# State update as 48-column tiles, and the state's output product as 64-row tiles in two PSUM banks

## The chip, the cores and the metric

One core of one Trainium2 chip. The metric is the device time of one execution in microseconds (us); lower is better. All runs that are compared are at a granted TensorE clock of 1.0 (0.997 to 0.999 in some executions).

## The reference

A gated linear attention over 4 batches, 8 heads, 768 tokens and head dimension D = 48, and after it a feed-forward block with a hard-swish:

```python
for t in range(S):
    state = alpha[:, :, t, :, None] * state + einsum('bhd,bhe->bhde', k[:, :, t], v[:, :, t])
    y[:, :, t] = einsum('bhd,bhde->bhe', q[:, :, t], state)
x = y.transpose(0, 2, 1, 3).reshape(3072, 384)
h = x @ w_in                        # 384 -> 2048
g = h * clip(h + 3, 0, 6) / 6
out = g @ w_out                     # 2048 -> 384
```

Everything is float32.

## The kernel before

The tokens go in 24 chunks of 128 (six per batch). Inside a chunk the recurrence is done by matrix products; between chunks a 48x48 state per head is carried on. Heads lie in pairs: on the 128 rows of a tile, head 0 of a pair has rows 0 to 47 and head 1 rows 64 to 111 (the rest is padding). Per chunk TensorE computes scores, an output product inside the chunk (`within`), the state's output product (`across`) and the state update (`update`). These are small against the feed-forward products around them, which fill most of the time.

```python
def bank(name, j):              # four PSUM banks in rotation, shared by all of these
    ps_t[name, j] = ps.tile([C, NP, C], FP, tag="t", bufs=4, name=name + "_ps")
    return ps_t[name, j]

def update(j):                  # 4 products, one per pair of heads: 128 columns by 96
    # ... (u is a bank seen as NP x 96 columns)
    for p in range(NP):
        one = vs[:, 2 * p]
        both = bass.AP(one.tensor, one.offset, [one.ap[0], (C - D, 2), (1, D)])
        nc.tensor.matmul(u[:, p], kb_t[j][:, p], both, start=True, stop=True)

def next_state(j):              # VectorE takes only the two diagonal 48x48 blocks of each pair
    # ...

def across(j):                  # 12 products in four tiles of 32 columns, all 128 rows
    # ...
    for n in range(KT * NP):
        kk, p = divmod(n, NP)
        nc.tensor.matmul(ps_t["y", j][32 * p : 32 * p + 32, kk],
                         st[j % 2][:, p, 32 * kk : 32 * kk + 32], Q_t[j][:, p],
                         start=False, stop=(kk == KT - 1), skip_group_check=True)

def keep_x(j):                  # ScalarE copies the output to SBUF
    # ...
    nc.scalar.copy(out=xT_t[g][:, :, (j % G) * C : (j % G + 1) * C],
                   in_=ps_t.pop(("y", j))[:, 0:KT])
```

The order of all instructions is written down by hand, as a string of some 1,600 words: `u.7` is the update of chunk 7, `yi.7` and `yx.7` its two output products, `st.8` the decayed state for chunk 8, `z` are filler products that keep TensorE busy during the start, `M`, `P`, `f` are the feed-forward.

```python
with tc.manual_schedule():
    run("""z.3.6 lk.0 lq.0 la.0 la.1 tk.0 w.1 tq.0 ta.0 ca.0 ta.1 r.0 z.0.18 ca.1 ...
```

## Time and profile before

| | before |
|---|---|
| time, median of 3 | 582.42 us (581.78 to 582.7) |
| span of the profiled execution | 579.1 us |
| TensorE busy | 568.0 us, 98% |
| TensorE instructions | 5112 |

The lines that show TensorE as the bound are in the prediction. The waits of TensorE (who waited for whom: us in total, times, longest):

```profile
PE m_ps L461 <- DVE ones L114: 4.2, 1, 4.2
PE ta_ps L267 <- DMA rings<-in_alpha_dram: 1.1, 1, 1.1
```

The first filler waits for the constant tile that it multiplies, and a transpose of an input (into `ta_ps`; `tk_ps` and `tq_ps` are others) for its transfer. The start has about 1.5 us more of such waits, and after it there is hardly any. The second is the timeline near 60 us (start, length, engine, line):

```profile
58.16 1.66 POOL L207 TENSOR_TENSOR w<-raw 128x768 int32<-128x768 int32 x1 [3.22 <-DVE raw L202]
...
59.00 1.13 PE L367 MATMUL u_ps<-t,kb 128*128 128x96 f32 x8
...
59.96 1.70 PE L420 MATMUL m_ps<-xT,w 128*128 128x256 f32 x7
```

GpSimd's last step on a weight piece ends at 58.16 + 1.66 = 59.82 us. The product that uses it starts at 59.96, and that product's weight load, which reads the piece, already at 59.88. There is no wait in the list, but the piece was only 0.14 us early for the product, and 0.06 us for its load.

### The profile page before, as it was taken

What the parts mean: (1) busy time and instruction counts of PE and PEld (TensorE: products, weight loads), DVE (VectorE), ACT (ScalarE), POOL (GpSimd) and SP (SyncE); (2) the same over time, 40 slices, a digit from 0 to 9 for tenths busy, and PEclk for the clock granted to TensorE, in tenths of its full rate; (3) what the DMA queues carried; (4) which work ended last, traced back from release to release, by engine and by line L of the source; (5) the groups of instructions that cost most, each with busy time, mean ns of one, the idle gap of its engine ahead of it and who ended that gap; (6) DMA issues with size and microseconds to landing.
All of it is one profiled execution on the core that took longest, in us unless ns stands there. A gap on an engine that the chain in (4) does not pass through costs nothing.

```text
span 579.1 us, 12352 instructions
## 1 busy us (share of the span) xinstructions
PE 568.0 (98%) x5112; PEld 531.3 (92%) x5112; DVE 473.4 (82%) x787; ACT 194.9 (34%) x335; POOL 53.2 (9%) x70
## 2 busy tenths in 40 slices
PE   6899999999999999999999999999999999999997
PEld 6788877699999999999999999999999999999997
DVE  5889889999999999895997886984998975655571
ACT  2346552103522523323323422422431431432420
POOL 2252435000000000000000000000000000000000
PEclk9999999999999999999999999999999999999999
DMA  9999797105115143440431331232242000000000
GB/s 166 202 177 211 213 236 177 37 23 140 33 40 141 28 99 75 97 103 8 97 79 32 78 90 40 58 96 54 48 113 46 16 23 8 1 22 8 3 18 28
DMA packets 87607, 45.83 MB, mean 79 GB/s; under 512 B 48896, under 2 KB 82432, under 8 KB 87552
## 3 DMA queue, kind: packets, MB, share of 16 engines
q1 hardware_dynamic: 80928, 40.33, 32.5%
q10 hardware_dynamic: 6624, 4.72, 2.4%
q8 instruction: 40, 0.66, 0.5%
q14 instruction: 15, 0.12, 0.1%
HBM read 40.30 MB, written 4.72 MB: 78 GB/s over the span
## 4 chain that ended last, share of the span: by engine, by line
PE 90%; DVE 4%; DMA 3%; SPq 2%; issue 1%; ACT 0%; DVEq 0%
PE m_ps L630 34%; PE m_ps L530 30%; PE m_ps L420 7%; PE sc_ps L325 4%; PE m_ps L446 4%; PE y_ps L389 3%; PE y_ps L399 2%; PE u_ps L367 2%; PE kb_ps L342 1%; DMA rings<-in_alpha_dram 1%; DMA raw<-in_moe_w_in_dram 1%; SPq L172 1%; DVE g_sb L428 1%; SPq L235 1%; DVE P L305 1%
## 5 line engine op out<-in xcount | busy, mean ns | idle before, releaser
L630 PE MATMUL m_ps<-w,g_sb 128*128 128x192 f32 x704 | 121.8, 328 | 0.5 <-DVE g_sb L467 0.3
L630 PEld LDWEIGHTS m_ps<-w,g_sb 128*128 128x128 f32 x704 | 113.7, 190 | 3.3 <-DVE g_sb L467 1.2
L536 ACT COPY g_sb<-m_ps 128x512 f32<-128x512 f32 x110 | 64.1, 584 | 118.3 <-PE m_ps L530 103.9
L630 PE MATMUL m_ps<-rings,g_sb 128*128 128x192 f32 x528 | 91.4, 326 | 0.5 <-DVE oh L646 0.5
L630 PEld LDWEIGHTS m_ps<-rings,g_sb 128*128 128x128 f32 x528 | 85.7, 190 | 0.8 <-DVE oh L646 0.7
L530 PE MATMUL m_ps<-xc,w 128*128 128x128 f32 x640 | 83.0, 277 | 0.3 <-DVE xc L467 0.3
L530 PEld LDWEIGHTS m_ps<-xc,w 128*128 128x128 f32 x640 | 77.8, 192 | 2.4 <-issue 1.8
L424 ACT ACTIVATE r<-g_sb,half 128x512 f32<-128x512 f32 x80 | 57.1, 723 | 60.6 <-DVE g_sb L469 22.6
L428 DVE SCALAR_TENSOR_TENSOR g_sb<-r,g_sb 128x512 f32<-128x512 f32 x80 | 55.4, 702 | 22.1 <-PE m_ps L630 13.5
L352 POOL TENSOR_TENSOR t<-t,R 128x384 f32<-128x384 f32 x20 | 19.4, 971 | 390.1 <-DVE t L379 213.9
L530 PE MATMUL m_ps<-xT,raw 128*128 128x128 f32 x400 | 52.8, 279 | 0.0
L530 PEld LDWEIGHTS m_ps<-xT,raw 128*128 128x128 f32 x400 | 48.4, 192 | 1.3
L530 PE MATMUL m_ps<-xT,w 128*128 128x128 f32 x320 | 44.1, 281 | 0.0
L420 PE MATMUL m_ps<-xT,w 128*128 128x256 f32 x192 | 43.6, 382 | 0.2 <-ACT xT L407 0.2
L577 DVE TENSOR_TENSOR g_sb<-g_sb 128x512 f32<-128x512 f32 (+1 forms) x55 | 41.9, 794 | 0.1
L530 PEld LDWEIGHTS m_ps<-xT,w 128*128 128x128 f32 x320 | 38.7, 191 | 3.2 <-ACT g_sb L536 1.4
L331 DVE TENSOR_TENSOR A<-sc_ps,mask 128x512 f32<-128x512 f32 x48 | 30.8, 684 | 12.5 <-PE sc_ps L325 12.4
L420 PEld LDWEIGHTS m_ps<-xT,w 128*128 128x128 f32 x192 | 35.8, 190 | 5.6 <-issue 0.4
L294 DVE TENSOR_TENSOR_SCAN R<-t,ones 128x516 f32<-128x516 f32 x24 | 29.4, 1224 | 8.0 <-ACT t L285 5.0
L530 PE MATMUL m_ps<-xc,raw 128*128 128x128 f32 x240 | 32.0, 276 | 0.0
L305 DVE TENSOR_TENSOR_SCAN P<-t 128x516 f32<-128x516 f32 x24 | 30.6, 1275 | 0.1
L467 DVE TENSOR_TENSOR g_sb<-g_sb 128x512 f32<-128x512 f32 x40 | 28.1, 703 | 2.9 <-ACT g_sb L536 2.6
(100 smaller groups left out, 714.1 us busy)
## 6 DMA issues: line engine op xcount, KB each, us to landing
raw<-in_moe_w_out_dram SPq DMA_DIRECT2D x8, 768.0 KB, 4.9
raw<-in_moe_w_in_dram SPq DMA_DIRECT2D x24, 192.0 KB, 6.9
t<-in_v_dram SPq DMA_DIRECT2D x48, 96.0 KB, 2.9
out_dram<-oh ACTq DMA_DIRECT2D x44, 96.0 KB, 2.2
qq<-in_q_dram SPq DMA_DIRECT2D x36, 96.0 KB, 2.4
aq<-in_alpha_dram SPq DMA_DIRECT2D x36, 96.0 KB, 2.5
kq<-in_k_dram SPq DMA_DIRECT2D x36, 96.0 KB, 2.5
qq<-in_q_dram SPq DMA_DIRECT2D x36, 80.0 KB, 2.5
```

Source lines behind the costliest of these rows:

```text
L294: nc.vector.tensor_tensor_scan(out=reverse(R, n - 1, n), data0=reverse(ax, n, n), data1=reverse(ones, n, n), initial=0.0, op0=ALU.mult, op ...
L305: nc.vector.tensor_tensor_scan(out=P_t[j], data0=aX[j % 2][:, 0:n], data1=ini[j % 2], initial=0.0, op0=ALU.mult, op1=ALU.add)
L325: nc.tensor.matmul(sc[h % 2][:, h // 2], K_t[j][r, h // 2], Q_t[j][r, h // 2], start=True, stop=True)
L331: nc.vector.tensor_tensor(out=A_t[j][:, NP * o : NP * (o + 1)], in0=ps_t.pop(("sc%d" % o, j)), in1=mask.unsqueeze(1).to_broadcast([C, NP, ...
L420: nc.tensor.matmul(h[:, f], w1[:, kk, o : o + C], xT_t[g][:, kk], start=(kk == 0), stop=(kk == KT - 1))
L424: nc.scalar.activation(out=to, in_=h, func=AF.Relu, bias=half, scale=1.0 / 6.0)
L428: nc.vector.scalar_tensor_tensor(out=to, in0=r, scalar=1.0, in1=h, op0=ALU.min, op1=ALU.mult)
L467: eng.tensor_tensor(out=out, in0=in0, in1=in1, op=ALU.add if s1 > 0 else ALU.subtract)
L530: nc.tensor.matmul(acc[g][i][:, f * C : (f + 1) * C], spots[w][:, f * C : (f + 1) * C], x_of(g, x), start=(first and f == 0), stop=last, s ...
L536: nc.scalar.copy(out=slots[z], in_=acc[g][i])
L577: nc.vector.tensor_tensor(out=out, in0=in0, in1=in1, op=ALU.subtract)
L630: nc.tensor.matmul(to[g], a, rhs[:, f], start=(first and f == 0), stop=(last and f == HF - 1), skip_group_check=True)
```

## The change

The intent: the update computes 128x96 per pair of heads, of which only two 48x48 blocks are used. Now it computes just these, as two column tiles side by side. In the state's output product, the outer thirds of the output belong to one head each, so half of their rows are zeros. Now they are 64 rows high, two above each other, in different PSUM banks (`y0` and `y1`). The middle third stays at full height. The copy to SBUF becomes two, and the order string was written anew.

```diff
     def update(j):
         for p in range(NP):
-            one = vs[:, 2 * p]
-            both = bass.AP(one.tensor, one.offset, [one.ap[0], (C - D, 2), (1, D)])
-            nc.tensor.matmul(u[:, p], kb_t[j][:, p], both, start=True, stop=True)
+            for a in range(2):
+                nc.tensor.matmul(u[64 * a : 64 * a + D, p, D * a : D * a + D],
+                                 kb_t[j][:, p, 64 * a : 64 * a + D],
+                                 vs[:, 2 * p + a, (64 - D) * a : (64 - D) * a + D],
+                                 start=True, stop=True)
...
+    def y_of(j, kk, p):
+        return ps_t["y%d" % (kk // 2), j][32 * p : 32 * p + 32, kk % 2]
...
     def across(j):
-        for n in range(KT * NP):
-            kk, p = divmod(n, NP)
-            nc.tensor.matmul(ps_t["y", j][32 * p : 32 * p + 32, kk],
-                             st[j % 2][:, p, 32 * kk : 32 * kk + 32], Q_t[j][:, p],
-                             start=False, stop=(kk == KT - 1), skip_group_check=True)
+        parts = [(p, 2 * a, slice(64 * a, 64 * a + 64)) for p in range(NP) for a in range(2)]
+        for p, kk, r in parts + [(p, 1, slice(0, C)) for p in range(NP)]:
+            nc.tensor.matmul(y_of(j, kk, p), st[j % 2][r, p, 32 * kk : 32 * kk + 32],
+                             Q_t[j][r, p], start=False, stop=(kk > 0), skip_group_check=True)
...
     def keep_x(j):
-        nc.scalar.copy(out=xT_t[g][:, :, (j % G) * C : (j % G + 1) * C],
-                       in_=ps_t.pop(("y", j))[:, 0:KT])
+        at = xT_t[g][:, :, (j % G) * C : (j % G + 1) * C]
+        nc.scalar.copy(out=at[:, 0:2], in_=ps_t.pop(("y0", j))[:, 0:2])
+        nc.scalar.copy(out=at[:, 2], in_=ps_t.pop(("y1", j))[:, 0])
...
-        run("""z.3.6 lk.0 lq.0 la.0 la.1 tk.0 w.1 tq.0 ta.0 ca.0 ta.1 r.0 z.0.18 ca.1 ...
+        run("""lk.0 lq.0 la.0 la.1 tk.0 w.1 tq.0 ta.0 ca.0 ta.1 r.0 z.0.18 ca.1 ...
         # the whole string is new, with 10 filler products fewer (30 instead of 40)
```

## The prediction

> **What bounds the kernel now.** I read the page first (shares, slices, chain), then the stretches by window, then TensorE's groups by form, and last its timeline in a steady part.
>
> ```profile
> PE 568.0 (98%) x5112; PEld 531.3 (92%) x5112; DVE 473.4 (82%) x787; ACT 194.9 (34%) x335; POOL 53.2 (9%) x70
> PE   6899999999999999999999999999999999999997
> DVE  5889889999999999895997886984998975655571
> PE 90%; DVE 4%; DMA 3%; SPq 2%; issue 1%; ACT 0%; DVEq 0%
> ```
>
> The reader is to see a TensorE that hardly ever stands still: it is 90% of the chain that ended last and fills every slice but the first and the last. ScalarE has two thirds of its time free. VectorE is less comfortable than its 82% looks, which the stretches show (columns: PE, PEld, DVE, ACT, POOL busy, then clock and DMA):
>
> ```profile
> 0.00:30.00 30.00, 22.94 (x254) 21.08 (x255) 22.09 (x40) 10.18 (x14) 8.18 (x26) 1.00 1.11 186
> 30.00:130.00 100.00, 100.00 (x728) 81.79 (x727) 91.54 (x129) 39.44 (x57) 30.28 (x30) 1.00 0.69 153
> 130.00:180.00 50.00, 49.71 (x445) 47.63 (x444) 49.74 (x88) 17.07 (x31) 2.08 (x2) 1.00 0.36 87
> 180.00:225.00 45.00, 45.00 (x461) 43.26 (x460) 43.53 (x75) 14.66 (x26) 1.67 (x2) 1.00 0.36 82
> 450.00:495.00 45.00, 45.00 (x432) 43.40 (x429) 33.25 (x61) 14.01 (x26) 1.67 (x2) 1.00 0.06 15
> ```
>
> The first 30 us are a start in which TensorE is idle for 7 us and also runs filler products. From 130 to 225 us both TensorE and VectorE are full (VectorE 49.74 of 50, then 43.53 of 45). Later TensorE alone is.
>
> The three groups that the change touches or leans on, in the view by form (busy time, then the mean of one):
>
> ```profile
> L367 PE MATMUL u_ps<-t,kb 128*128 128x96 f32 x160 | 21.0, 274 | 0.2 <-ACT kb L347 0.2
> L399 PE MATMUL y_ps<-q,t 128*32 128x128 f32 x480 | 17.2, 277 | 0.0
> L389 PE MATMUL y_ps<-A,t 128*32 128x128 f32 x768 | 25.9, 275 | 0.0
> ```
>
> Each float32 product stands as two instructions (80 products of the state update are x160). The means of 274 to 277 ns include the pipeline and are no cost. The cost is the distance from start to start, which the timeline gives (start, length, line, count):
>
> ```profile
> 229.78 1.03 PE L367 MATMUL u_ps<-t,kb 128*128 128x96 f32 x8
> 230.65 2.02 PE L530 MATMUL m_ps<-xc,w 128*128 128x128 f32 x16
> 232.60 1.08 PE L389 MATMUL y_ps<-A,t 128*32 128x128 f32 x32
> 233.62 1.16 PE L530 MATMUL m_ps<-xT,w 128*128 128x128 f32 x8
> 234.70 0.86 PE L399 MATMUL y_ps<-q,t 128*32 128x128 f32 x24
> 235.50 1.16 PE L530 MATMUL m_ps<-xT,w 128*128 128x128 f32 x8
> 236.49 2.77 PE L630 MATMUL m_ps<-w,g_sb 128*128 128x192 f32 x16
> ...
> 245.19 1.05 PE L530 MATMUL m_ps<-xc,w 128*128 128x128 f32 x8
> 246.08 0.39 PE L530 MATMUL m_ps<-xc,raw 128*128 128x128 f32 x2
> ```
>
> The update takes about 0.87 to 0.89 us for 8, so 111 ns each. That is the pace of a 128-column weight load (eight of L530 from 245.19 to 246.08: 0.89 us), not of its 96 moving columns. The two tiled groups take 1.02 us for 32 and 0.80 us for 24. Their difference, 0.22 us for two rounds of four, says that four column tiles run together and a round costs 109 ns. What is left over (1.02 - 8 x 0.109 = 0.15 us), plus what the L530 group before and after a tiled group takes above 0.89 us (1.08 before one, 0.99 between the last and L630), gives about 0.33 us for going into a tiled group and out again.
>
> **What the Trainium skill says.** (1) "TensorEngine Tiling (Array Packing)", Key Properties: changing the tiling mode, not only the tile, drains TensorE. The trace agrees: the first weight load of a new mode starts 0.20 us after the last 128-column product started, against 0.11 us inside a mode; so a drain costs about 95 ns beyond the stream. (2) "TensorE: Matmul & The Clock Gate", LDWEIGHTS: the load's time follows the number of columns P, about P/1.2 ns, whatever the rows. 128 columns give 107, the trace's pace is 111; 48 columns give an estimate of 40 ns, which nothing in this trace shows. (3) The tiling page, Gotcha 1, says that different row tiles cannot use one PSUM bank at the same time; this explains the second bank, and no run here shows it yet. (4) Its section Instruction Overhead puts about 60 cycles on each matmul; if that were a floor of some 50 ns (60 columns at the trace's 0.83 ns), a 48-column product would not quite scale.
>
> **The change part by part.** The order of the changed kernel's instructions, compared engine by engine, gives the counts.
>
> State update. Removed: 4 products of 128 weight columns by 96. Added: 8 of 48 by 48, in two column tiles. Before: 8 instructions x 111.7 = 0.894 us per chunk. After: 16 instructions in 8 rounds of two. A round is estimated at 48 x 0.83 + 5 = 45 ns (weights and stream both 40, the second load under the first product), so 0.36 us. For 20 chunks: 17.9 to 7.2, -10.7 us.
>
> Output product of the state. Before 6 rounds of 109 = 0.654 us per chunk. After: 8 half-height tiles of 64 rows by 32 columns together (2 rounds, if rows and columns combine), then the middle third at full height (2 rounds): 0.436 us. For 20 chunks -4.4 us. That row tiles combine is shown by the score products, whose 16 half-height instructions take 1.09 us with both changes of mode, so they run in pairs.
>
> Changes of mode. I counted them in both orders: 131 before, 182 after. Returns to the whole array go from 65 to 76; each costs 95 + 107 - 3 = 0.199 us, since the first 128-column load lies bare: +2.2 us. New entries into 64x32 tiles: 20 x (95 + 27) = +2.4 us. New entries into 128x64 tiles: 20 x (95 + 40) = +2.7 us. Together +7.3 us. The entries to the 32-column mode stay at 42, because the middle third is a new entry each time but the outer thirds take over the old one.
>
> Sum on TensorE: -10.7 - 4.4 + 7.3 = -7.8 us. As a check, the same counting (rounds, loads and changes, without idle) gives 562.9 us for the kernel before; its span is 579.1, 9.3 of the missing 16 us lie before 30 us and about 3 are spread over the rest.
>
> What doesn't reach the end: in the first 30 us TensorE waits for others anyway, so two updates and one output product there don't count (-0.8 us of gain). From 130 to 225 us VectorE has only 1.7 us free, and the work for it is unchanged. About seven of twenty chunks' gain (7 x 0.39 = 2.7 us) falls between 30 and 225 us; I let half of it be lost, 1.4 us. Ten filler products fewer (2.2 us of TensorE time) fall in the start, where they filled idle time: 0.
>
> Evacuation. The copy of the output becomes two: from the trace, 128x384 took 470 ns, 128x512 584 and 128x192 318, so 256 and 128 columns together are an estimate of 635 ns, +0.165 us for 24 chunks, 4 us on a ScalarE that is 66% idle. Two of the four shared PSUM banks now go to one output, so waits for a bank get likelier; the order was laid out anew for it. I take 0.5 us for both.
>
> Total: -7.8 + 0.8 + 1.4 + 0.5 = about -5.1 us, and 582.4 - 5.1 = 577.3 us.
>
> **The rivals.** (a) The switches eat it all. If going from 64-row to 128-row tiles, or in and out of 64-column tiles, drains longer than the 95 ns seen (say twice), 51 extra changes cost another 5 us: 582. Against it: all changes seen before, of three kinds, cost the same. (b) Small products don't scale: a round of the update at 60 ns or more instead of 45 takes back 2.4 us; if the two tiles didn't overlap at all (16 x 45), 7.2 us: about 584. Against: four column tiles overlap perfectly in the rows shown. (c) Eight tiles of 64x32 don't run together, but four and four: +4.4 us, about 581.5. (d) VectorE or the banks become the bound: the whole gain before 225 us and some waits later are lost: 579 to 581. For it: VectorE's 99% between 130 and 180 us. (e) The upside: no drain between 64x32 and 128x32 (-2.4 us) and VectorE following at no loss (-1.4 us): 573.5.
>
> **Range and chances.** The centre is 577.3 us, 0.9% under before. Two of the downward surprises together reach 573, one or two of the upward ones 581.5. For over 2% faster it would have to be under 571, more than the whole TensorE sum without any loss; for over 2% slower over 594, which needs several rivals at once. So: faster 0.03, same 0.95, slower 0.02.
>
> **What would show each step right or wrong.** The update's 16 instructions should take about 0.36 us from first to last start (0.70 or more means no overlap). The 16 half-height output instructions should start in two groups of eight 109 ns apart, and the middle third about 0.2 us after the last of them. TensorE's busy share should stay at 98%, with DVE about the same busy time and ACT about 4 us more. In windows of steady work after 225 us the gain per chunk should be near 0.39 us; between 130 and 225 us less, with TensorE waiting for VectorE tiles. I am wrong if TensorE's idle time grows by more than 3 us, or if the start takes longer than the 30 us of before.

## More of the kernel before

The weights come as 16 pieces, and each is converted before use by a chain of ScalarE (L187, L191), VectorE (L198, L200, L202) and GpSimd (L207):

```python
def add_low(i):                 # L207, the last step for weight piece i
    dst, lo, hi = slice_of(i)
    nc.gpsimd.tensor_tensor(out=dst.bitcast(I32), in0=hi.bitcast(I32), in1=lo.bitcast(I32), op=ALU.add)
```

## The result, and the profile after

| | before | after |
|---|---|---|
| time, median | 582.54 us (4 runs) | 578.6 us (4 runs, 577.22 to 579.17) |
| ratio of the fast runs | | 0.9931 (95%: 0.991 to 0.9953) |
| span, profiled execution | 579.1 us | 575.4 us |

A ratio is the mean time of one kernel's fast runs over that of the other's of the same rounds, so it is not quite the ratio of the medians. Here: 0.7% faster, which counts as the same (the line is 2%). The output is correct.

The page of the changed kernel: busy times, and the chain that ended last.

```profile
PE 561.5 (98%) x5252; PEld 515.3 (90%) x5252; DVE 472.4 (82%) x787; ACT 195.8 (34%) x359; POOL 50.1 (9%) x70
PE 84%; DVE 6%; DMA 4%; SPq 4%; issue 1%; ACT 1%; DVEq 0%; ACTq 0%
```

TensorE is busy 6.5 us less, but the span shrank by 3.7 us only. TensorE's idle time grew from 579.1 - 568.0 = 11.1 to 13.9 us. And its share of the chain fell from 90 to 84%: other engines and transfers now take part in setting the end.

The stretches of the changed kernel (columns as in the prediction):

```profile
0.00:30.00 30.00, 22.30 (x254) 18.70 (x255) 23.00 (x42) 10.47 (x16) 9.24 (x26) 1.00 1.10 179
30.00:130.00 100.00, 97.58 (x736) 76.67 (x734) 90.20 (x127) 39.38 (x62) 27.31 (x30) 1.00 0.70 155
130.00:180.00 50.00, 49.81 (x470) 47.84 (x470) 49.37 (x87) 16.17 (x31) 1.67 (x2) 1.00 0.35 82
180.00:225.00 45.00, 44.85 (x485) 41.99 (x484) 44.07 (x74) 16.45 (x31) 2.09 (x2) 1.00 0.35 82
```

Between 30 and 130 us TensorE stood at 100.00 of 100 before; now 2.4 us of idle time are there. The waits say for what:

```profile
PE tk_ps L267 <- DMA rings<-in_k_dram: 4.8, 2, 4.2
PE ta_ps L267 <- DMA rings<-in_alpha_dram: 2.0, 2, 1.6
PE m_ps L426 <- POOL w L207: 1.1, 1, 1.1
```

Most of the first two lines lies before 30 us. The 2.4 us are 0.6 for `tk_ps`, 0.3 for VectorE's masked scores, 0.4 for ScalarE at 128 us, and the last line: a feed-forward product waits 1.1 us for a converted weight, which is new. The timeline shows that chain from its transfer on (cut: L191 and the three steps of VectorE):

```profile
55.22 0.95 ACT L187 ACTIVATE raw<-raw 128x768 int32<-128x768 uint32 x1 [2.98 <-DMA raw<-in_moe_w_in_dram]
...
59.59 1.46 POOL L207 TENSOR_TENSOR w<-raw 128x768 int32<-128x768 int32 x1 [3.89 <-DVE raw L202]
...
61.11 1.56 PE L426 MATMUL m_ps<-xT,w 128*128 128x256 f32 x6 [1.10 <-POOL w L207]
```

ScalarE had stood idle for 2.98 us until the weight piece landed. Then six steps on three engines follow, and TensorE, done with its small products at about 60 us, waits until 61.11.

The groups themselves did become cheaper. By form:

```profile
L365 PE MATMUL u_ps<-t,kb 128*48 128x48 f32 x320 | 11.6, 213 | 0.8 <-ACT kb L347 0.8
L405 PE MATMUL y_ps<-q,t 64*32 64x128 f32 x320 | 9.0, 281 | 0.0
```

As in the kernel before, the means contain the pipeline. The cost is from start to start. An update and a state product from the middle of the kernel:

```profile
272.22 0.56 PE L365 MATMUL u_ps<-t,kb 128*48 128x48 f32 x16
272.71 1.16 PE L536 MATMUL m_ps<-xT,w 128*128 128x128 f32 x8
...
281.12 0.81 PE L405 MATMUL y_ps<-q,t 64*32 64x128 f32 x24
281.85 1.41 PE L636 MATMUL m_ps<-w,g_sb 128*128 128x192 f32 x7
```

From the update's start to the next group's 0.49 us pass, and some 0.1 us goes into the way in (271.23 to 272.22: eight products of 111.7 ns would take 0.89). The update before took 0.87 to 0.89 us, without a change of mode. The records of single instructions show how: the first pair starts at 272.217, from the second on pairs start every 45 ns (272.298, 272.343, 272.388, ... 272.568 us), the first and the last instruction are 357 ns apart, and the next group's weight load starts 136 ns after the last. In the state product, eight 64-row products start within 47 ns from 281.117 on and the next eight from 281.249 on (132 ns later and not 109, as the first eight wait for their weights; in 32-column groups it is 133). The middle third's first load begins at 281.494, 197 ns after the last of these. So eight tiles do run together, and going from 64 to 128 rows does drain.

### A counting model, and where the time went

To see where the gain was lost, I counted TensorE's work from the order of its instructions alone: 111.7 ns for a 128-column load, 109 ns for a round of 32-column tiles, 45 ns for a round of the update, 95 ns for each drain, and the first load of a new mode (27, 40 or 107 ns). The paces are read from the two traces, except for the first loads: these are worked out from 0.83 ns a column (products of 192 and 256 columns start every 163 and 216 ns). In the traces the first round of a mode takes 24, 35 or 101 ns longer than the next. This gives 562.9 us for the kernel before and 552.8 us after (131 and 182 changes of mode; 2.2 us of the difference are the ten fillers). Then I looked up when the same feed-forward product (the n-th in order) starts in two traces. Where the counted gain grows and the time doesn't, gain is lost. The experiments below use this.

### The profile page after: what moved, and what is told of

Its sections match the earlier page's. It is cut to its first block, busy times and chain, and to the rows that moved or that the text cites. A ratio compares the mean times of both kernels' runs of the same rounds, so it can differ in the third digit from the quotient of the medians.

```text
span 575.4 us, 12646 instructions
## 1 busy us (share of the span) xinstructions
PE 561.5 (98%) x5252; PEld 515.3 (90%) x5252; DVE 472.4 (82%) x787; ACT 195.8 (34%) x359; POOL 50.1 (9%) x70
## 4 chain that ended last, share of the span: by engine, by line
PE 84%; DVE 6%; DMA 4%; SPq 4%; issue 1%; ACT 1%; DVEq 0%; ACTq 0%
PE m_ps L636 33%; PE m_ps L536 30%; PE m_ps L426 4%; PE m_ps L452 4%; PE sc_ps L325 4%; PE y_ps L395 3%; DMA raw<-in_moe_w_in_dram 2%; PE y_ps L405 2%; SPq L235 1%; SPq L172 1%; PE u_ps L365 1%; PE m_ps L467 1%; PE kb_ps L342 1%; DVE g_sb L434 1%; DMA rings<-in_alpha_dram 1%
## 5 line engine op out<-in xcount | busy, mean ns | idle before, releaser
L536 PE MATMUL m_ps<-xT,w 128*128 128x128 f32 x320 | 42.7, 281 | 0.0
L473 DVE TENSOR_TENSOR g_sb<-m_ps,g_sb 128x512 f32<-128x512 f32 x30 | 20.4, 680 | 13.1 <-ACT g_sb L542 11.0
```

Of the source, the lines that this page charges most:

```text
L536: nc.tensor.matmul(acc[g][i][:, f * C : (f + 1) * C], spots[w][:, f * C : (f + 1) * C], x_of(g, x), start=(first and f == 0), stop=last, s ...
```

## The experiments

Theory A, the prediction's own, is that the count on TensorE decides, less a loss at the start and where VectorE is full. The rivals are that the new order costs time and the products gain more than counted, that the mode changes eat the row tiles' gain, and that the start is held up by the transfers and hides the gain. The kernel before ran beside them on the same chip; its median was 581.76 us beside e1 to e4, 581.51 us beside e5 to e8, and 581.42 us beside e9 to e12.

### e1: the new update alone, in the old order

```diff
  (kernel before, with only this changed, order untouched)
-            nc.tensor.matmul(u[:, p], kb_t[j][:, p], both, start=True, stop=True)
+            for a in range(2):
+                nc.tensor.matmul(u[64 * a : 64 * a + D, p, D * a : D * a + D], ...
```

> The kernel before with the state update alone changed, in the instruction order of before. Counting theory (TensorE's rounds and mode changes set the time): update 17.9 to 7.2 us, changes of mode 131 to 165 (+5.4 us), so 5.2 us off TensorE's work, of which 0.5 to 0.8 us lie in the start and don't count: 577.9 to 578.3 us against 582.5. Rival, VectorE full between 130 and 225 us: another 1 us or more is lost, 579 to 580. Rival, the changed order is what gains: close to 582.

Measured: 579.16 us (5 runs), ratio 0.9956 (0.9944 to 0.9969), correct; span 577.2 us. The count gave -5.25 us, so about half of it arrived. At the product that starts at 55 us the count is -1.4 and the time -0.46 us; at 228 us -3.0 and -0.58; at the end -5.25 and -1.85 (in the traces). Of the seven updates after 330 us five bring the 0.20 us that the count says, and two bring nothing. So the update's count is right in most places where TensorE alone is the limit, and most of the early gain is not had.

### e2: the new output product alone, in the new order

```diff
  (changed kernel)
     def update(j):
-            for a in range(2): ...
+            nc.tensor.matmul(u[:, p], kb_t[j][:, p], both, start=True, stop=True)
```

> The changed kernel with the old state update, in the new order. Counting theory: against the kernel e3 (new order, no change of the products) the output product gains 13.1 - 8.7 = 4.4 us and pays 2.4 us for 20 more changes of mode: about 2.0 us under e3. If e3 is at 585 this is at 583, that is, not faster than before at all. Rival, half-height tiles cost or save something else than the count (waits for the second bank): over 1 us away from that.

Measured: 581.66 us, ratio 0.9997 (0.9984 to 1.0009), correct; span 579.2 us. By itself the new output product brings nothing that can be seen in the time. To read this right, the next run is needed.

### e3: neither product, only the new order

```diff
  (kernel before: its products and its copy)
-        run("""z.3.6 lk.0 lq.0 la.0 ...     # order of before
+        run("""lk.0 lq.0 la.0 la.1 ...      # order of after
```

> The products of before in the instruction order of the changed kernel: only the order differs from before. Theory: the new order's start costs about 2.5 to 2.8 us (the lag of TensorE behind its counted work is 9.4 us at 62 us in before and 14.4 us in the changed kernel, of which 2.2 us are the ten filler products left out), the rest next to nothing: 585 to 586 us. Rival: the order is neutral, 582 to 583, and the loss in the changed kernel's start came from the new products or banks.

Measured: 581.48 us, ratio 0.9993 (0.9981 to 1.0006), correct; span 579.7 us. The expectation of a slow order (585 us and over) fell. The order is neutral: its count is 2.0 us lower, mostly the fillers left out, and what its span has beyond the count is larger (18.8 us against 16.2). So the change's gain is the products' gain, and e3 is the right partner for the changed kernel, since both have the same order. Against e3, e2's span is 0.5 us shorter, of 2.0 us counted.

The same products in e3 and in the changed kernel:

| the product starts, in the changed kernel (us) | counted gain (us) | gain in time (us) |
|---|---|---|
| 30.25 | 0.90 | 0.70 |
| 47.35 | 1.60 | 1.22 |
| 61.11 | 2.10 | 0.10 |
| 130.81 | 2.50 | 0.41 |
| 246.17 | 4.51 | 1.60 |
| 398.33 | 6.32 | 2.83 |
| 554.51 | 8.03 | 4.32 |

Of the 3.7 us that are lost, 2.0 are lost by 61 us. The gain that was had at 47 us is gone at 61.11. That is the product that waits for GpSimd in the changed kernel. In e3, GpSimd and that product:

```profile
59.69 1.47 POOL L207 TENSOR_TENSOR w<-raw 128x768 int32<-128x768 int32 x1 [3.92 <-DVE raw L202]
61.21 1.99 PE L420 MATMUL m_ps<-xT,w 128*128 128x256 f32 x8
```

The weight was ready at 61.16 and TensorE came at 61.21. It hardly waited: its weight load started 0.27 us after the one before it, where 0.11 is the pace, too little for the list. With the cheaper products TensorE comes early and waits, for a weight that is ready at nearly the same time (59.59 + 1.46 = 61.05).

### e4: outer thirds at full height again

```diff
  (changed kernel)
-        parts = [(p, 2 * a, slice(64 * a, 64 * a + 64)) for p in range(NP) for a in range(2)]
+        parts = [(p, 2 * a, slice(0, C)) for a in range(2) for p in range(NP)]
```

> The changed kernel with the outer thirds as full-height tiles again (128 rows, two banks kept, order kept). Counting theory: 6 rounds in place of 4 (+4.4 us) and 20 changes of mode fewer (-2.4 us): 2.0 us slower than the changed kernel, about 580.6. Rival, the change between 64x32 and 128x32 is dear or row tiles gain nothing: the same 578.6 or faster.

Measured: 578.71 us, ratio 0.9951 (0.9937 to 0.9964), correct; span 577.0 us. The changed kernel has ratios of 0.9931 and (e9) 0.9946, so the row tiles are worth between 0.3 and 1.2 us of the 2.0 counted; by the spans it is 1.6 (1.1 against e9's). This is less sure than the update's part, because the start scatters: in the profiled execution of e9, which is the changed kernel once more, the product of 61.11 us starts at 61.63. With e2 the picture is: the update brings most of the gain, the row tiles a little. Past the start the traces agree better: from 61 us to the end the changed kernel gains 0.96 us on e4, and e2 gains 0.96 on e3, of 1.63 counted both times. What is missing is the change from 64 to 128 rows: from the first product of the 64-row tiles to the first of the middle third 379 ns pass in each of the 20 chunks, where 340 are counted, and for the 17 chunks of this stretch that is 0.7 us.

### e5 and e10: half of three weight loads left out

Is it the transfers that hold the product at 61 us? Of the weight pieces 5 to 7 only half of the rows are loaded. The result is wrong; TensorE's work is the same.

```diff
  (changed kernel)
-            for p in range(NP):
+            for p in range(NP // 2 if 5 <= i < NW1 else NP):
                 nc.sync.dma_start(out=to[32 * p : 32 * p + 32], in_=src[p])
```

> The changed kernel with the last three pieces of the first weight matrix loaded by half (64 of 128 rows; wrong result on purpose). Theory: up to 62 us the arrival of the weights sets the pace, so the new products' gain there is lost (TensorE's lag grows from 11.7 to 14.4 us between 30 and 62 us, against 11.4 to 12.4 in e3). With 1.2 MB less to load the wait for the weights near 61 us goes away and the lag at 62 us is about 12.5: 1.5 to 2 us faster, 576.6 to 577.1. Rival, VectorE and GpSimd's conversion of the weights or the order is the limit, not the loading: unchanged at 578.6.

Measured: 576.28 us, ratio 0.9903 (0.9886 to 0.9919) over its three fast runs. Its profiled execution is of no use: 814.98 us at a granted clock of 0.659.

> The same kernel as e5, whose profile fell in a slow execution (clock 0.66), for a profile at full clock and a comparison on the chip of e9. Theory: TensorE's wait of 1.1 us for the weights near 61 us is gone and the point that stands at 61.1 us in the changed kernel comes 1.5 to 2 us earlier; 1.5 to 2 us faster than e9 in all. Rival (conversion or order is the limit): that point stays at about 61 us and the time is that of e9.

Measured: 575.82 us, ratio 0.9901 (0.9885 to 0.9918); span 573.2 us, clock 1.0. In the timeline:

```profile
56.27 1.46 POOL L207 TENSOR_TENSOR w<-raw 128x768 int32<-128x768 int32 x1 [2.71 <-DVE raw L202]
...
58.73 3.50 PE L426 MATMUL m_ps<-xT,w 128*128 128x256 f32 x15
```

The weight is ready at 57.73 us, a microsecond before it is wanted. The wait for GpSimd has gone from the list, the product starts at 58.73 instead of 61.11, and those 2.4 us stay to the last product (0.65 of them are there at 47 us, before these pieces are used). The span is 2.2 us shorter than the changed kernel's and 2.7 us shorter than e9's, more than the 1.5 to 2 us expected. So the start, up to 61 us, is set by the weights' transfers and their conversion; what TensorE saves before that doesn't reach the end. That the table's first losses are this is argued: the weight was ready at 61.16 in e3 and at 61.05 in the changed kernel, so in neither could the product start earlier. Whether e3 with halved loads would have gained as well was not tried.

### e9: the changed kernel again

No edit; the control for e10 to e12.

> The changed kernel once more, as the control on the same chip for the three runs beside it: 0.993 of before, 577.5 to 578.6 us.

Measured: 578.65 us, ratio 0.9946 (0.9932 to 0.9961), correct; span 575.9 us. It repeats the result, slightly weaker. Its trace repeats the table past the start: against e3 it is 0.4 us behind at the product of 61 us, and from there to 554 us it gains 4.2 us of 5.9 counted, as the first profile did.

### e6: the start of the old order

The first 159 words of the old order, then the rest of the new one.

```diff
  (changed kernel)
-        run("""lk.0 lq.0 la.0 la.1 tk.0 w.1 tq.0 ta.0 ...
+        run("""z.3.6 lk.0 lq.0 la.0 la.1 tk.0 w.1 tq.0 ta.0 ...
```

> The changed kernel with the first part of the order (up to the last product of the first layer's first group) as in before, the rest as in the changed kernel; both parts hold the same work. Theory: the start of before has the weights ready at about 59.5 us in place of 61.1: 1.2 to 1.6 us faster than the changed kernel, about 577.2. Rival, the start is bound by bandwidth whatever the order: 578.6.

Measured: 576.32 us (6 runs, 575.26 to 579.26), ratio 0.9912 (0.9891 to 0.9933), correct; span 575.0 us. The old start is no worse, and by the ratios better by 1 to 2 us; by the profiled executions only by 0.4. It has ten fillers more, which cost nothing here: they lie in time that TensorE has anyway. This speaks for the same cause as e10. The wait for GpSimd's weight is 0.7 us in it.

### e7: the two output products joined

The way into a tiled group and out again costs about a third of a microsecond, so it should pay to do both output products of a chunk next to each other. Here the inner one moves down to the state's, which takes its middle third first (the same mode as the inner product).

```diff
  (changed kernel; 17 chunks like this one)
-  h.4.0 yi.10 sm.10 o.4.1.0 M.4.18.2 st.11 lv.13.1 ca.12 e.4.1 M.4.10 n.4.18.9 h.4.1 yx.10 o.4.6.0
+  h.4.0 sm.10 o.4.1.0 M.4.18.2 st.11 lv.13.1 ca.12 e.4.1 M.4.10 n.4.18.9 h.4.1 yi.10 yx.10 o.4.6.0
...
-        for p, kk, r in parts + [(p, 1, slice(0, C)) for p in range(NP)]:
+        for p, kk, r in [(p, 1, slice(0, C)) for p in range(NP)] + parts:
```

> The changed kernel with each chunk's inner output product moved to stand right before its output product of the state (from the fifth chunk on), middle third first, so that both share one stay in the 32-column mode. Counted: 182 to 152 changes of mode, 4.8 us less: 573.8. Rival, the steady part is held by VectorE and ScalarE too, which wait for the later output copy: half or less of it, 576 or more.

Measured: 582.11 us, ratio 1.0011 (0.9997 to 1.0025); span 579.9 us. The result is wrong: in six chunks the load of a later chunk's `v` into the same buffer now stood ahead of the product that reads it (`lv.13` ahead of `yi.10` above). The time is still of use, since no product is seen waiting for such a load. All that the 30 saved changes of mode should bring is lost, and more: the count is 4.7 us lower than the changed kernel's, the span 4.5 us longer. The waits name half of it:

```profile
PE m_ps L536 <- ACT g_sb L542: 4.6, 8, 0.7
```

```profile
380.83 1.06 PE L536 MATMUL m_ps<-xc,raw 128*128 128x128 f32 x8
382.56 1.16 PE L536 MATMUL m_ps<-xc,w 128*128 128x128 f32 x8 [0.68 <-ACT g_sb L542]
383.65 1.08 PE L395 MATMUL y_ps<-A,t 128*32 128x128 f32 x32
```

Three feed-forward groups of 0.9 us now stand in a row, and the third waits for ScalarE to copy a bank out. In the changed kernel a tiled group stood between them (the inner product at 380.24 us) and gave ScalarE that time. The tiled groups also serve as spacers. What the other half of the loss is was not looked into.

### e8: old start, joined products, six updates joined too

```diff
  (e6, and e7's moves, and for chunks 8, 10, 14, 16, 20, 22, like this one)
-  h.4.1 yi.10 yx.10 o.4.6.0 ...
+  h.4.1 u.10 yi.10 yx.10 sm.10 o.4.6.0 ...
```

> e6 and e7 together, and six state updates moved next to the joined output products: counted 5.8 us less than e6, so 571 to 572 us, 1.8% under before. Rival as in e7: 574 or more.

Measured: 582.24 us, ratio 1.0015 (1.0 to 1.003), span 579.9 us. Wrong for e7's reason, and because the decayed state of a later chunk stood ahead of the update that it needs (`st.15` ahead of `u.14`). With the start of e6 as a base the loss is 4.9 us in the span: moving groups down does not pay.

### e11: the state's product moved up to the inner one

The other way round: `yx` moves up to stand right after `yi`, in the 16 chunks from 4 on where the state is decayed by then (not in chunk 7). The inner product stays where it was, so no spacer is taken away there.

```diff
  (e6; 16 chunks like this one, and the middle third first as in e7)
-  h.4.0 yi.10 sm.10 o.4.1.0 M.4.18.2 st.11 lv.13.1 ca.12 e.4.1 M.4.10 n.4.18.9 h.4.1 yx.10 o.4.6.0
+  h.4.0 yi.10 yx.10 sm.10 o.4.1.0 ...
```

> The start of before (as e6), and from the fifth chunk on the output product of the state moved up to stand right after the inner one, middle third first, so that both share a stay in the 32-column mode; nothing is moved down, so no load of v is overtaken as in e7. Counted: 179 to 155 changes of mode, 3.7 us less than e6: about 572.8 us, 1.5% under before. Rival, as e7 showed: TensorE's gain turns into waits for copies out of PSUM, at least half is lost: 575 or more.

Measured: 573.01 us (4 runs, 572.82 to 573.84), ratio 0.9855 (0.984 to 0.9869), correct; span 570.7 us. This is the best kernel: 8.4 us under the kernel before (1.45%, still under the line of 2%), 5.6 us under e9 on the same chip, of which 1 to 2 came with the old start (e6). Against e6 the count is 3.7 us lower and the last product comes 4.3 us earlier; 0.8 of the 4.3 is there at 61 us, up to where both have almost the same work and order, so it is probably scatter of the start.

```profile
276.09 1.08 PE L395 MATMUL y_ps<-A,t 128*32 128x128 f32 x32
276.99 0.78 PE L405 MATMUL y_ps<-q,t 128*32 128x128 f32 x24
277.70 1.16 PE L536 MATMUL m_ps<-xT,w 128*128 128x128 f32 x8
```

From the inner product's start to the state product's 0.90 us pass instead of 1.01 when a full-width group follows, and there is one way in and one way out fewer. ScalarE is hardly waited for as in e7: that line of the waits is 0.2 us in all.

### e12: e11 with eight updates moved next to them

```diff
  (e11; for chunks 8, 10, 14, 16, 20, 22 like this one; 9 and 21 after yx)
-  h.4.0 yi.10 yx.10 sm.10 o.4.1.0
+  h.4.0 u.10 yi.10 yx.10 sm.10 o.4.1.0
```

> e11 with eight state updates moved next to the joined output products: counted 1.6 us less than e11, 571.5 us. Rival: the moved updates leave TensorE without spacers between products that wait for a bank of PSUM to be copied out, no faster than e11.

Measured: 574.66 us, ratio 0.988 (0.9866 to 0.9895), span 572.3 us. Slower than e11, though the count is 1.6 us lower. It is also wrong: `st.15` and `st.23` stood ahead of the updates `u.14` and `u.22`. The new order would need these moved too, and I had no reason left to, as it gains nothing.

What could not be tried: the new output product in the old order. Two banks per output in flight locked up with that order in the simulator, with the new update and without. So the change as a whole was not split from its order in that direction.

## Why the prediction was right or wrong

The prediction (577.3 us) was right in its class and its range, and 1.3 us too low against 578.6. By its own steps:

- **The update, 45 ns a round, -10.7 us.** Right. Its pairs start 45 ns apart. That the first and last instruction are 357 ns apart, where 0.36 us was predicted, is partly luck: eight rounds have seven distances, and the first is 81 ns, as the first pair waits for its weights. Rival (b), small products that don't scale, fell.
- **The state product, two rounds of eight, then the middle third, -4.4 us.** Right as to the mechanism; rival (c) fell. In the time it is worth little: e2 none, e4 between 0.3 and 1.2 us, and in the traces 0.96 us past the start, of 1.63 counted.
- **The changes of mode, +7.3 us.** Right in kind: the drain between 64 and 128 rows is there, so the upside of (e) is not, and the changes in and out of 64-column tiles cost no more than others, so most of (a) is not either. One change was counted too cheap: from 64x32 to 128x32, by 40 ns, which is 0.8 us for 20 chunks. Probably part of it is that the eight starts of a round spread over 47 ns and those of four over 20, which the count leaves out.
- **The sum, -7.8 us.** Against e3, which has the same order, the count is -8.03.
- **The start, "in the first 30 us", 0.8 us lost.** This is the term that was mis-sized most. The start that doesn't count lasts to 61 us and takes 2.0 us of the gain (2.5 in e9's trace). I took its end from the slices and the window, where TensorE is full from 30 us on. It is full, but of work that had to come out just when the weights did: the piece used at 59.96 us had been ready for 0.14 us. A busy engine with a deadline beside it isn't free to gain. e10 shows the deadline, by moving it. The DMA engines' share had shown it too: it is 1.04 over the first 62 us of the kernel before, and the prediction's stretch from 30 to 130 us, with 0.69, hid that. Of the prediction's own signs, "if the start takes longer than the 30 us of before" is met in this sense: the product of 59.96 us starts at 61.11 in the changed kernel, and the old start in e6 brings it to 60.26.
- **VectorE, 1.4 us, and the banks, 0.5 us.** From 61 us on, 1.7 us of 5.9 counted are lost, against 1.9 estimated: the size is about right, but mostly by luck. TensorE has no more idle time between 130 and 225 us than before (0.34 us against 0.29), and waits for VectorE tiles, which I named as the sign, are not among its longest waits. Of the 1.7 us, 0.9 are lost between 61 and 246 us, where VectorE is full for the most part, and 0.8 after it, where it isn't; a chunk gains 0.30 us there, not 0.39. The traces tell what takes them: about 0.7 is the change of mode that was counted too cheap, and about 1.0 four short pauses between weight loads (at 210.6, 232.6, 320.4 and 345.1 us; the third is 0.2 us longer than in e3, the others e3 doesn't have, and e9 has all four, half a microsecond later). The profile puts the second and third, 0.4 us, down to VectorE (L477), and names nothing for the other two.
- **The fillers and the new order, 0.** Right in the sum: e3, which leaves the fillers out, has the time of the kernel before. Its start is slower, though (the product of 59.96 us comes at 61.21), and e6, with the old start and the fillers, is 1 to 2 us faster by the ratios.
- **ScalarE, +4 us.** The copies took 369 and 273 ns, 642 together against 635 estimated, so 15.5 us against 11.3. ScalarE's busy time grew by 0.9 us only, because it counts overlapping records once: the sum of its instructions' times grew by 4.0 us (205.3 to 209.3). The list of TensorE's waits for it has 1.2 us, as in e3 (before: 0.4), so the copies cost nothing that shows.
- **Idle time of TensorE** grew by 2.8 us, just within the 3 us that were to prove me wrong.

So: -8.0 counted, 2.0 lost by 61 us and 1.7 after it, leaves 4.3 us at the product of 554.51 us; the span gives 4.3 against e3 and 3.7 against before, the medians 3.9.

## What to carry to other kernels

Where an engine is full from some moment on, look for the transfer or conversion that arrives just in time for it, before booking a saving there: a wait that is absent because it is 0.14 us short of existing will take the saving. Small tiled products are paid to about half in changes of mode (by the count 0.33 us beside 0.36 for an update, 0.44 beside 0.44 for a state product; all 182 together are about 30 us), so once they are small, put those of the same row and column size next to each other. Which of the two is moved matters: here it paid to move the later one up (e11) and not the earlier one down (e7), so keep the tiled groups that give another engine the time to empty the banks.

## What the Trainium skill lacked or had wrong

- "TensorEngine Tiling (Array Packing)", Key Properties, says that a change of mode drains TensorE, and gives no figure. Here about 200 ns pass from the start of the last product of 128 moving columns to the first weight load of the next mode, and 136 ns after one of 48 columns; that is about 95 ns beyond the stream. Then the first weight load lies bare: the first round takes 24, 35 or 101 ns longer than the next, for 32, 48 or 128 weight columns. A change of the row height alone counts as well: 197 ns passed between the last 64x32 product and the first 128x32 load, against about 110 ns from round to round.
- The same page, Instruction Overhead, says that a product with a free dimension of 1 has the latency of one with 60. It doesn't say how long a cycle is. For throughput no floor of 50 ns (60 columns at 0.83 ns) shows here: 48 columns in two column tiles repeat every 45 ns, and two instructions start in that time.
- "TensorE: Matmul & The Clock Gate", "Wait — 56ns, not 53.3ns?", says that starts are never closer than about 25 ns. For products in different tiles of the array they are: 5 to 8 ns here, as a figure further down the page (Measured speedup vs the span model, about 4 ns a tile) would let one expect.
- The same page, The mechanism, says that weight loads overlap products in flight "only when row_grp differs" (the paragraph ahead of it also allows the background weight buffer). In the update both tiles have all 128 rows, and a load starts 2 ns after a product of its rows started (272.298 and 272.300 us), 206 ns before that product's recorded (modelled) end.
- No page says that a tiled group between full-width groups can serve as the time in which a bank is emptied: taking them out from there cost the joined kernel 4.6 us of waits on ScalarE (e7).
